# S4D convolution and gated linear unit on one core: which queues issue the output stores, and where the last Fourier stage stands

## The chip, the cores and the metric

The kernel runs on one core of a Trainium2 chip. The metric is device time in microseconds (us) of one execution, as a median over runs. Engines are called as in the profile: PE is TensorE's matmul, PEld its weight load, DVE is VectorE, ACT ScalarE, POOL GpSimd, SP SyncE. DMAs are issued by SP, ACT and POOL; a "q" behind an engine's name means its instruction queue (waits and DMA issues).

## The reference

The input has 2048 tokens of 448 channels. Both branches read the same layer-normalised input, and their outputs are added to the input:

```python
def _A_ref(u, log_A_real, A_imag, C_real, C_imag, log_dt, D_skip):
    ...
    P = jnp.exp((A * dt[:, None])[:, :, None] * pos[None, None, :])
    K = 2.0 * jnp.einsum("dn,dnl->dl", C, P).real
    Kf = jnp.fft.rfft(K, L2)
    Uf = jnp.fft.rfft(u_t, L2)
    y = jnp.fft.irfft(Uf * Kf[None, :, :], L2)[:, :, :L]
    return y + u * D_skip[None, None, :]

def _B_ref(x, w_gate, w_up, w_down):
    h = _sigmoid(einsum(x, w_gate)) * einsum(x, w_up)
    return einsum(h, w_down)

xn = _layernorm(x)
return x + _A_ref(xn, ...) + _B_ref(xn, ...)
```

A is a convolution over the whole sequence with a kernel K that is itself computed (448 channels, 256 states); B is a gated linear unit with 1792 inner features.

## The kernel before, in words

**Two streams, one order.** `conv()` does branch A and `glu()` branch B. Both are Python generators that write instructions and yield a cost; the loop at the end of the kernel always advances the stream that is behind by its share of the total, so their instructions are interleaved on every engine by those costs. `tc.issue_after` ties a group of matmuls behind the other stream's last one, which fixes the order on TensorE.

**Branch B (`glu`).** The 2048 tokens are 16 blocks of 128 (b 0 to 15), in two halves of eight. A half has two tiles of four blocks (t = 0, 1). For groups of two or three weight blocks f, `gate` (L710) multiplies tokens by the gate and up weights, ScalarE takes a tanh (`th`, L718), VectorE forms `hf` (L721), ScalarE rounds it to `hh` (L726), VectorE keeps the rest `hl`. Then come eight *down blocks*, one for each (t, b): nine matmuls for a group of three (`po`, L823) and one add into the accumulator on VectorE (`acc`, L828). In the second half GpSimd loads some of the weights and splits them in a high and a low part (`wh`, `wl` from `wraw`; `dh`, `dl` from `rdw`, L794 and L795). The accumulators of the first half go to DRAM and come back as `ac` (blocks 0 to 7); those of the second half are `accs[2]` (blocks 8 to 11) and `accs[3]` (12 to 15).

**Branch A (`spectra`).** The convolution is done by Fourier stages of 64 x 64, for the two halves of the channels apart (h = 0, 1: 224 columns each, H = 224). For each of 17 steps (h, k): `there` transforms kernel and input (`sp`, L904), ScalarE copies the kernel's part out of PSUM (`kc`, L912), VectorE multiplies (`yy`, `pd`, L915 to L918), `back` transforms back (`pv`, L931), ScalarE copies to `vt` (L937), which goes to DRAM (`v_d`) and returns in another layout (`vp`, L953). The loads of a step (`skl`, `sx`, `tb`) are issued by SP three steps ahead. `last(h, m)` is the last Fourier stage of a column half: 32 matmuls in the program (`pv`, L964; the two calls with m = 0, 2 or 4, 6 together are one row x64 in the trace) and adds into the accumulators (L972). m = 0, 2 finish `ac`, m = 4, 6 finish `accs[2]` and `accs[3]`. For h = 0 they are called in `spectra`, two in one step and two in the next. For h = 1 they are called in `glu`, between the last group's down blocks.

**Stores.** `out` (L234) writes four blocks and one column half by four DMAs of 32 partitions, 4 tokens and 224 columns (112 KB each). The issuing queue goes round: SP, ACT, POOL, by a counter (L238). The eight stores of `ac` for h = 0 are issued in the middle of the Fourier steps, all others at the end: h = 0 of `accs[2]` behind the down blocks of t = 0, then `ac` h = 1 behind `last(1, 0)` and `last(1, 2)`, `accs[3]` h = 0 behind the last down block, and at last `accs[2]` and `accs[3]` h = 1.

**Semaphores.** A DMA announces that it has landed on a semaphore. SP's and ACT's DMAs share eight of them (DMAHW0 to DMAHW7), POOL's have eight of their own (DMASW0 to 7). A DMA whose semaphore was used by an earlier one waits in its queue until that one has landed, and whatever is behind it in the queue waits too.

Of the kernel before, what the change touches and what calls it, by code (L numbers as in the profile page):

```python
# [20 lines left out]
D = 448  # L21
# [18 lines left out]
H = D // 2  # L40
# [90 lines left out]
def s4d_glu_kernel(ctx, tc, io):  # L131
    nc = tc.nc
# [4 lines left out]
    x_t, out_t = tok(io["A_u"][0]), tok(io["out"][0])  # L137
# [91 lines left out]
    accs = [acc_tile() for _ in range(2)]  # L229

    def blocks(t, g, b0, nb):
        return t[g, :, b0 // 8, b0 // 4 % 2, b0 % 4 : b0 % 4 + nb]

    def out(src, b0, h):  # L234

        ds = slice(H * h, H * h + H)
        for g in range(4):
            eng = (nc.sync, nc.scalar, nc.gpsimd)[outs[0] % 3]  # L238
            outs[0] += 1
            eng.dma_start(blocks(out_t, g, b0, 4)[:, :, ds], src[32 * g : 32 * g + 32, :, ds])  # L240

    def x_load(dst, b0, nb, engs):
        for g in range(4):
# [487 lines left out]
    def glu():  # L731
        for half in range(2):
# [4 lines left out]
            for fs_ in ORDER[half]:  # L737
# [3 lines left out]
                final = half == 1 and fs_ is ORDER[1][-1]  # L741
# [64 lines left out]
                for t in range(2):  # L806
                    acc = accs[2 * half + t]
                    for b in range(4):
                        if final and (t, b) == (0, 1):

                            yield None
                        if final and (t, b) == (1, 2):

                            sp_mm[:] = glu_mm
                            for m in (0, 2):
                                lasts[0](1, m)
                        po = psg.tile([128, D], F32, name="po", tag="gu", bufs=4)
                        bs = slice(128 * b, 128 * b + 128)
                        n = 0
# [13 lines left out]
                            step(*downs[t, b])  # L833
                    if cross:
                        nc.sync.dma_start(acc_d[:, 4 * t : 4 * t + 4], acc)
                    if final:
                        out(acc, 8 + 4 * t, 0)
                if final:
                    sp_mm[:] = glu_mm
                    for m in (4, 6):  # L840
                        lasts[0](1, m)
                    for t in range(2):
                        out(accs[2 + t], 8 + 4 * t, 1)

    def spectra(pf):

# [108 lines left out]
        def last(h, m):  # L955
# [13 lines left out]
            for b in range(2):  # L969
                q, o, ds = 2 * (m // 4) + b, m % 4, slice(H * h, H * h + H)  # L970
                acc = ac[:, 4 * q + o : 4 * q + o + 2, ds] if q < 2 else accs[q][:, o : o + 2, ds]
                v.tensor_tensor(acc, acc, pos[b], ALU.add)  # L972
# [135 lines left out]
            yield from spectra(pf)  # L1108

    turns = []  # L1110
    lasts, glu_mm, sp_mm, glu_on, outs, x1s, hfs, xls = [], [], [], [], [0], [0], [], []
# [45 lines left out]
```

## Time and profile before

| | |
|---|---|
| median of 3 runs | 721.07 us (721.0 to 723.01) |
| the profiled execution | 721.87 us, span 720.1 us |
| busy PE / PEld | 670.9 / 527.3 us (93% / 73% of the span) |
| busy DVE / ACT / POOL | 551.4 / 428.0 / 371.5 us (77% / 59% / 52%) |
| DMA | 117.23 MB, 163 GB/s over the span |

The span runs from the first to the last instruction; the execution's own time is 1.8 us longer. A row of the timeline has the start, the duration, engine, line, operation, output and inputs, the number of instructions merged in it, and in brackets the idle time ahead of it with what ended it. A row of the table of stretches has the stretch, its length, then busy time (and count) of PE, PEld, DVE, ACT and POOL, TensorE's granted clock, the busy share of the DMA engines and GB/s. A row of a line's instructions has durations as shortest/median/longest in ns, then the first and last start.

### The profile page before, as it was taken

The numbers are of one execution on the slowest core, as the hardware profiler recorded it, in microseconds if no ns is written. First come the engines' busy times: TensorE is split into PE (matmuls) and PEld (weight loads), VectorE is DVE, ScalarE is ACT, GpSimd is POOL, SyncE is SP. The second block draws the span as 40 slices with busy tenths as digits, with TensorE's granted clock in tenths as the row PEclk, the third lists the DMA queues.
The fourth block names the chain that finished last, engine by engine and source line by source line (L and its number), as shares of the span: only waits on it lengthen the run. The fifth ranks groups of instructions, "written<-read, shape, count | busy, mean of one in ns | idle before, by whom it ended". The sixth has DMA issues, their size and how long they took to land.

```text
span 720.1 us, 19127 instructions
## 1 busy us (share of the span) xinstructions
PE 670.9 (93%) x7752; PEld 527.3 (73%) x7752; DVE 551.4 (77%) x766; ACT 428.0 (59%) x678; POOL 371.5 (52%) x431
## 2 busy tenths in 40 slices
PE   3898999999997997989999999999999999998995
PEld 2676888877876875656888788877877777776783
DVE  5899988699899889985879889987946555546543
ACT  3655975677787789965686877777542322313320
POOL 2100147766987988885676687577833002251001
PEclk9999999999999999999999999999999999999998
DMA  9947374554254453647933344141359988899645
GB/s 208 238 118 215 97 214 154 166 159 153 64 168 140 135 135 107 178 136 203 257 112 95 95 132 128 46 140 43 86 162 319 216 235 231 253 290 228 172 131 152
DMA packets 94503, 117.23 MB, mean 163 GB/s; under 512 B 12752, under 2 KB 78288, under 8 KB 94416
## 3 DMA queue, kind: packets, MB, share of 16 engines
q1 hardware_dynamic: 65904, 91.87, 45.3%
q10 hardware_dynamic: 25936, 18.24, 9.5%
q0 software_dynamic: 2576, 5.90, 3.1%
q8 instruction: 61, 1.00, 0.6%
q14 instruction: 26, 0.21, 0.1%
HBM read 72.13 MB, written 43.84 MB: 161 GB/s over the span
## 4 chain that ended last, share of the span: by engine, by line
PE 42%; DVE 6%; ACT 4%; DMA 3%; issue 2%; SPq 1%; POOL 0%; POOLq 0%; DVEq 0%; ACTq 0%
PE gu L710 16%; PE po L823 9%; PE sp L904 6%; PE pv L931 4%; PE ko L616 4%; PE tr L542 2%; DVE Ft L604 1%; DMA sx<-x_d 1%; DVE Et L602 1%; DMA out_dram<-ac 1%; DVE Et L603 1%; PE kp L566 1%; ACT S L551 1%; ACT S L548 1%; SPq L492 1%
## 5 line engine op out<-in xcount | busy, mean ns | idle before, releaser
L520 POOL TENSOR_TENSOR me<-me,pm 128x32 f32<-128x32 f32 (+1 forms) x168 | 142.4, 848 | 73.4 <-DVE Et L603 62.1
L520 POOL TENSOR_TENSOR mf<-mf,pm 128x64 f32<-128x64 f32 (+1 forms) x112 | 119.7, 1069 | 5.9
L710 PE MATMUL gu<-xh,wh 128*128 128x512 f32 x336 | 100.0, 406 | 0.7 <-ACT xh L221 0.7
L710 PE MATMUL gu<-xh,wl 128*128 128x512 f32 x336 | 97.0, 395 | 0.0
L710 PE MATMUL gu<-xl,wh 128*128 128x512 f32 x336 | 95.8, 391 | 0.0
L602 DVE TENSOR_TENSOR Et<-me,S 128x1024 f32<-128x1024 f32 x56 | 81.8, 1461 | 17.2 <-ACT S L551 16.1
L603 DVE TENSOR_TENSOR Et<-me,S 128x1024 f32<-128x1024 f32 x56 | 78.0, 1394 | 12.6 <-ACT me L533 10.5
L823 PE MATMUL po<-dh,hh 128*128 128x448 f32 x224 | 84.2, 376 | 2.6 <-DVE hf L721 2.2
L823 PE MATMUL po<-dl,hh 128*128 128x448 f32 x224 | 82.3, 367 | 0.0
L604 DVE TENSOR_TENSOR Ft<-mf,S 128x1024 f32<-128x1024 f32 x56 | 78.1, 1394 | 5.4 <-ACT S L551 2.7
L548 ACT ACTIVATE S<-tr 128x1024 f32<-128x1024 f32 x56 | 57.6, 1028 | 40.8 <-PE tr L542 40.4
L823 PE MATMUL po<-dh,hl 128*128 128x448 f32 x224 | 81.2, 367 | 0.0
L616 PEld LDWEIGHTS ko<-Et,Ft 128*32 128x32 f32 x3584 | 55.2, 112 | 31.4 <-DVE Ft L604 13.3
L710 PEld LDWEIGHTS gu<-xh,wh 128*128 128x128 f32 x336 | 61.8, 191 | 20.1 <-issue 5.1
L616 PE MATMUL ko<-Et,Ft 128*32 128x64 f32 x3584 | 65.6, 224 | 10.8 <-DVE Ft L604 9.9
L710 PEld LDWEIGHTS gu<-xh,wl 128*128 128x128 f32 x336 | 63.8, 190 | 14.5 <-DVE hf L721 0.7
L710 PEld LDWEIGHTS gu<-xl,wh 128*128 128x128 f32 x336 | 63.4, 189 | 13.5
L726 ACT CAST hh<-hf 128x512 fp32r<-128x512 f32 x56 | 34.9, 623 | 61.8 <-DVE hf L721 57.7
L721 DVE SCALAR_TENSOR_TENSOR hf<-th,gu 128x512 f32<-128x512 f32 x56 | 38.1, 680 | 39.5 <-PE gu L710 27.1
L551 ACT ACTIVATE S<-S,hpi 128x1024 f32<-128x1024 f32 x56 | 65.5, 1170 | 0.0
L787 POOL TENSOR_TENSOR dl<-rd,dh 128x448 fp32r<-128x448 f32 x14 | 24.8, 1769 | 78.1 <-ACT dh L786 67.6
L828 DVE SCALAR_TENSOR_TENSOR acc<-po,acc 128x448 f32<-128x448 f32 x80 | 48.1, 615 | 20.7 <-PE po L823 20.4
(208 smaller groups left out, 1299.7 us busy)
## 6 DMA issues: line engine op xcount, KB each, us to landing
sk_d<-sk ACTq DMA_DIRECT2D x14, 512.0 KB
sx<-x_d SPq DMA_DIRECT2D x32, 224.0 KB
skl<-sk_d SPq DMA_DIRECT2D x16, 448.0 KB
vp<-v_d SPq DMA_DIRECT2D x16, 448.0 KB
v_d<-vt SPq DMA_DIRECT2D x14, 448.0 KB
ph<-ph_d SPq DMA_DIRECT2D x224, 24.0 KB
wt_d<-wh SPq DMA_DIRECT2D x9, 512.0 KB
wt_d<-wl SPq DMA_DIRECT2D x9, 512.0 KB
```

The costliest lines, as they stand in the source:

```text
L520: ins = nc.gpsimd.tensor_tensor(m[:, :, w + a : 2 * w : n], m[:, :, a:w:n], par(base + i).unsqueeze(2).to_broadcast([128, 4 * DC, w // n]) ...
L548: nc.scalar.activation(rows(cs), pv, AF.Abs)
L551: sins[:] = [nc.scalar.activation(cs, cs, AF.Sin, scale=-TWO_PI, bias=hpi)]
L602: v.tensor_tensor(Et[:, :, :, 32:64], two(me[:, :, 32:64]), S[:, 1::-1], ALU.mult)
L603: v.tensor_tensor(Et[:, :, :, 0:32], two(me[:, :, 0:32]), S[:, 1:3, :, ::-1], ALU.mult)
L604: fts[:] = [v.tensor_tensor(Ft, two(mf), S[:, 3:5], ALU.mult)]
L616: mm = nc.tensor.matmul(ko[32 * j : 32 * j + 32, sl], Ft[:, cc, DC * h + 4 * q + j], Et[:, cc, DC * h + 4 * q + j], start=(k == 0), stop=( ...
L710: glu_mm[:] = [nc.tensor.matmul(ps, a_, b_, start=(n == 0), stop=(n == len(mm) - 1))]
L721: marks[1] = v.scalar_tensor_tensor(hf, th, 1.0, pgu[1], ALU.add, ALU.mult)
L823: glu_mm[:] = [nc.tensor.matmul(po, a_[:, bs], w_, start=(n == 0), stop=(n == 3 * fc - 1))]
L828: v.scalar_tensor_tensor(acc[:, b], po, 0.5, acc[:, b], ALU.mult, ALU.add)
L904: mm = nc.tensor.matmul(to, tb[:kk, t, 64 * c : 64 * c + 64], rhs, start=True, stop=True, skip_group_check=True,)
```

## The change

`out` no longer goes round: it takes the range of blocks, the columns and the queues.

```diff
-    def out(src, b0, h):
-        ds = slice(H * h, H * h + H)
+    def out(src, b0, nb, ds, engs):
         for g in range(4):
-            eng = (nc.sync, nc.scalar, nc.gpsimd)[outs[0] % 3]
-            outs[0] += 1
-            eng.dma_start(blocks(out_t, g, b0, 4)[:, :, ds], src[32 * g : 32 * g + 32, :, ds])
+            eng = engs[g % len(engs)]
+            eng.dma_start(blocks(out_t, g, b0, nb)[:, :, ds], src[32 * g : 32 * g + 32, b0 % 4 : b0 % 4 + nb, ds])
...
-                        if final and (t, b) == (1, 2):
+                        if final and t == 1 and b >= 2:
                             sp_mm[:] = glu_mm
-                            for m in (0, 2):
+                            for m in (4 * b - 8, 4 * b - 6):
                                 lasts[0](1, m)
+                            if b == 3:
+                                out(accs[2], 8, 4, slice(H, D), (nc.sync, nc.scalar))
+                                out(accs[3], 12, 3, slice(0, D), (nc.sync, nc.scalar))
...
-                    if final:
-                        out(acc, 8 + 4 * t, 0)
-                if final:
-                    sp_mm[:] = glu_mm
-                    for m in (4, 6):
-                        lasts[0](1, m)
-                    for t in range(2):
-                        out(accs[2 + t], 8 + 4 * t, 1)
+                    if final and t == 0:
+                        out(acc, 8, 4, slice(0, H), (nc.gpsimd,))
+                    elif final:
+                        out(acc, 15, 1, slice(0, D), (nc.sync, nc.scalar))
...
                 for q in range(2):
-                    out(ac[:, 4 * q : 4 * q + 4], 4 * q, h)
+                    out(ac[:, 4 * q : 4 * q + 4], 4 * q, 4, ds, (nc.sync, nc.scalar) if h else (nc.gpsimd,))
```

The stores of column half 0 of `ac` and of `accs[2]` are issued by GpSimd alone, the others by SP and ACT in turn. `last(1, 4)` and `last(1, 6)` stand ahead of the last down block (t, b) = (1, 3); behind it only block 15 is left to store, with all its columns (four DMAs of 56 KB), and blocks 12 to 14 go out with all their columns as well (four of 168 KB). The lines below these places are two or three lower in the changed kernel (L240 is L238, L964 is L961).

On ScalarE (ACT), at the step in which `ac` is finished for h = 0, stood, with the semaphores that each instruction waits for:

```order
L912 COPY kc<-sp 128x448 [waits PE_49,Activation_49] x2
L240 DMA out_dram<-ac 32x4x224 [waits DMAHW4_49,DVE_49]
L240 DMA out_dram<-ac 32x4x224 [waits DMAHW7_49,DVE_49]
L240 DMA out_dram<-ac 32x4x224 [waits DMAHW1_49]
L718 ACTIVATE th<-gu 128x512 [waits PE_49]
L726 CAST hh<-hf 128x512 [waits DVE_49]
L937 COPY vt<-pv 128x2x224 [waits DMAHW2_49,PE_49]
```

and now stands:

```order
L909 COPY kc<-sp 128x448 [waits PE_49,Activation_49] x2
L716 ACTIVATE th<-gu 128x512 [waits PE_49]
L724 CAST hh<-hf 128x512 [waits DVE_49]
L934 COPY vt<-pv 128x2x224 [waits DMAHW2_49,DMAHW1_49,PE_49]
L934 COPY vt<-pv 128x2x224 [waits PE_49]
```

The three stores are gone, and `th`, `hh` and `vt` follow the copies `kc` directly. On GpSimd (POOL) at the same place and from there to the end, before:

```order
L648 DMA rdw<-in_B_w_down_dram 128x448 [waits Pool_49]
L240 DMA out_dram<-ac 32x4x224 [waits DMAHW4_49,DMAHW3_49,DVE_49]
L240 DMA out_dram<-ac 32x4x224 [waits DMAHW6_49,DMAHW5_49,DVE_49]
L794 CAST dh<-rdw 128x448 [waits DMASW2_49]
L795 TENSOR_TENSOR dl<-rdw,dh 128x448 [waits Pool_49]
L240 DMA out_dram<-acc 32x4x224 [waits DVE_49]
L240 DMA out_dram<-acc 32x4x224
L240 DMA out_dram<-ac 32x4x224 [waits DVE_49] x2
L240 DMA out_dram<-acc 32x4x224 [waits DVE_49]
L240 DMA out_dram<-acc 32x4x224
L240 DMA out_dram<-acc 32x4x224 [waits DMASW3_49,DVE_49]
L240 DMA out_dram<-acc 32x4x224 [waits DMASW4_49,DVE_49]
```

and now:

```order
L646 DMA rdw<-in_B_w_down_dram 128x448 [waits Pool_49]
L238 DMA out_dram<-ac 32x4x224 [waits DMAHW4_49,DMAHW3_49,DVE_49]
L238 DMA out_dram<-ac 32x4x224 x3
L238 DMA out_dram<-ac 32x4x224 [waits DMAHW6_49,DMAHW5_49,DVE_49]
L238 DMA out_dram<-ac 32x4x224 x2
L238 DMA out_dram<-ac 32x4x224 [waits DMASW2_49]
L792 CAST dh<-rdw 128x448
L793 TENSOR_TENSOR dl<-rdw,dh 128x448 [waits Pool_49]
L238 DMA out_dram<-acc 32x4x224 [waits DMASW3_49,DVE_49]
```

Eight stores instead of two stand ahead of the casts `dh` and `dl`, and the last of the eight takes over the wait for `rdw`. Behind `dl` GpSimd has four stores left (of `accs[2]`, h = 0) where it had eight, and none of them waits for the last Fourier stage. On ScalarE at the very end, where SP has the same rows, now stands:

```order
L238 DMA out_dram<-ac 32x4x224 [waits DMAHW7_49,DVE_49]
L238 DMA out_dram<-ac 32x4x224 [waits DMAHW1_49]
L238 DMA out_dram<-acc 32x4x224 [waits DMAHW2_49,DVE_49]
L238 DMA out_dram<-acc 32x4x224 [waits DMAHW5_49]
L238 DMA out_dram<-acc 32x1344 [waits DMAHW7_49,DVE_49]
L238 DMA out_dram<-acc 32x1344 [waits DMAHW1_49]
L238 DMA out_dram<-acc 32x448 [waits DMAHW3_49,DVE_49]
L238 DMA out_dram<-acc 32x448 [waits DMAHW5_49]
```

The two stores of block 15 (32x448) wait for the semaphores of stores of `accs[2]` that were issued eight DMAs earlier on the two queues. On TensorE the 32 rows of `last(1, 4)` and `last(1, 6)` stand nine matmuls further forward, between the last two down blocks.

More of the change, by code (lines that the diff above doesn't have):

```diff
@@ L1110, in s4d_glu_kernel @@
     turns = []
-    lasts, glu_mm, sp_mm, glu_on, outs, x1s, hfs, xls = [], [], [], [], [0], [0], [], []
+    lasts, glu_mm, sp_mm, glu_on, x1s, hfs, xls = [], [], [], [], [0], [], []
     xq, psc, raws, acl, marks, slots, pqs = list(x_first), [], [], [], [None, None], {}, []
```

## The prediction

> **What bounds the kernel now.** I read the page first, then TensorE's and ScalarE's timelines over the last 90 us, then the waits of the end. The page's head and its table of engines:
>
> ```profile
> span 720.1 us, 19127 instructions
> ...
> PE 670.9 (93%) x7752; PEld 527.3 (73%) x7752; DVE 551.4 (77%) x766; ACT 428.0 (59%) x678; POOL 371.5 (52%) x431
> ```
>
> TensorE is busy for 93% of the span, so a store matters only where it keeps TensorE waiting, or behind TensorE's last matmul. Both places exist. The first is the step in which the first Fourier half is finished. TensorE's timeline of an ordinary step with a `last` in it (from its `back`, line L931, at 631.55 to the next gate matmul, L710, at 639.09), then of the step after the stores:
>
> ```profile
> 631.55 1.78 PE L931 MATMUL pv<-yy,bk 64*128 64x224 f32 x16
> ...
> 639.09 0.97 PE L710 MATMUL gu<-xh,wh 128*128 128x512 f32 x3
> ...
> 644.31 1.78 PE L931 MATMUL pv<-yy,bk 64*128 64x224 f32 x16
> ...
> 650.36 0.98 PE L904 MATMUL sp<-skl,tb 128*64 128x224 f32 x8 [2.61 <-ACT vt L937]
> ...
> 654.38 0.96 PE L964 MATMUL pv<-vp,wf 64*32 64x224 f32 x16 [0.64 <-DVE pd L916]
> 655.27 0.96 PE L710 MATMUL gu<-xh,wh 128*128 128x512 f32 x3
> ```
>
> The brackets are idle time and what ended it: 2.61 us for ScalarE's copy `vt`, then 0.64 us for VectorE. Both steps run the same matmuls. The ordinary one takes 639.09 - 631.55 = 7.54 us, this one 655.27 - 644.31 = 10.96 us. ScalarE's timeline says why `vt` is late (its queue's DMA issues, taken from three narrow windows, then its instructions):
>
> ```profile
> 641.17 0.36 ACTq L240 DMA_DIRECT2D out_dram<-ac  x1
> ...
> 644.18 0.36 ACTq L240 DMA_DIRECT2D out_dram<-ac  x1
> ...
> 647.54 0.32 ACTq L240 DMA_DIRECT2D out_dram<-ac  x1
> 647.91 0.60 ACT L718 ACTIVATE th<-gu 128x512 f32<-128x512 f32 x1 [11.53 <-DMA out_dram<-ac]
> ...
> 649.79 0.96 ACT L937 COPY vt<-pv 128x448 f32<-128x448 f32 x2
> ```
>
> Three issues of about 0.35 us are spread from 641.17 to 647.86. Between them ScalarE's queue stands: the order shows a wait on a DMA semaphore (DMAHW7, DMAHW1) on the second and third store, that is, on the landing of an earlier transfer. `th`, `hh` and `vt` are queued behind. Was TensorE held by anything after that? One row of the table of stretches, 655.30 to 690.70:
>
> ```profile
> 655.30:690.70 35.40, 35.40 (x261) 26.64 (x258) 17.93 (x37) 11.69 (x22) 0.00 (x0) 1.00 0.77 179
> ```
>
> TensorE (second number) is busy for all 35.40 us at full clock (the 1.00), with the DMA engines 0.77 busy. So what is saved before 655 arrives in full at the down blocks.
>
> The second place is the end: TensorE's and VectorE's last instructions, the last issues of SP and ScalarE, then the rows of the kernel's closing line (L1153), where every engine waits for the others.
>
> ```profile
> 703.94 1.74 PE L964 MATMUL pv<-vp,wf 64*32 64x224 f32 x64
> 705.61 0.47 PE L823 MATMUL po<-dh,hh 128*128 128x448 f32 x1
> ...
> 707.33 0.37 PE L823 MATMUL po<-dh,hl 128*128 128x448 f32 x1
> ...
> 709.44 1.74 PE L964 MATMUL pv<-vp,wf 64*32 64x224 f32 x64
> ```
>
> ```profile
> 705.02 2.22 DVE L972 TENSOR_TENSOR ac<-ac,pv 128x448 f32<-128x448 f32 x4 [0.35 <-PE pv L964]
> 707.73 0.62 DVE L828 SCALAR_TENSOR_TENSOR acc<-po,acc 128x448 f32<-128x448 f32 x1 [0.50 <-PE po L823]
> 709.55 0.62 DVE L828 SCALAR_TENSOR_TENSOR acc<-po,acc 128x448 f32<-128x448 f32 x1 [1.20 <-PE po L823]
> 710.52 2.21 DVE L972 TENSOR_TENSOR acc<-acc,pv 128x448 f32<-128x448 f32 x4 [0.35 <-PE pv L964]
> ```
>
> ```profile
> 710.20 3.64 SPq L240 DMA_DIRECT2D out_dram<-acc  x4
> ```
>
> ```profile
> L1153 SPq EVENT_SEMAPHORE  x11: 17/28/3095, 713.9 to 720.0; - x11
> ...
> L1153 POOLq DRAIN  x3: 46/102/6277, 713.0 to 719.8; - x3
> L1153 SPq DRAIN  x3: 7/7/7, 717.8 to 719.6; - x3
> ...
> L1153 ACTq EVENT_SEMAPHORE  x2: 17/17/17, 719.5 to 720.0; - x2
> ```
>
> SP waits for the landings from 713.9 and has seen the last at 717.8, where its first DRAIN stands. GpSimd's first DRAIN begins at 713.0, right behind its last store, and the longest of the three lasts 6.28 us: to 719.3. The others are released at 719.5 and the span ends at 720.1. The end is thus set by GpSimd's own drain, 1.5 us behind the last landing, though no row of the chain of waits says so.
>
> **The change, part by part.**
>
> *The first half's stores leave SP and ScalarE.* ScalarE loses three issues with their waits, SP three. `th` can start when its matmuls end, `vt` when `pv` ends, as in the ordinary step, so the step should take 7.54 us: 10.96 - 7.54 = **3.4 us** saved on TensorE, the 2.61 us wait and what it drags behind it. Lower bound 2.6, the one wait that names ScalarE. More than 3.4 isn't there, since the rest of the step is matmuls that stay.
>
> SP's queue is relieved too: its next command, a `v_d` store, waits for `vt` anyway. The same 0.9 MB (8 x 112 KB) go through the same DMA engines, only later, so loads issued around 650 may land later; they fill buffers three steps ahead, and TensorE waited for none of them above. I take nothing for it.
>
> *GpSimd gets eight stores where it had two.* They stand behind the load of `rdw` and ahead of the casts `dh` and `dl`. GpSimd's timeline there, and the first matmul that uses the group's `dh` and `dl`:
>
> ```profile
> 647.33 1.16 POOL L240 DMA_DIRECT2D out_dram<-ac  x2
> 650.73 0.56 POOL L794 CAST dh<-rdw 128x448 fp32r<-128x448 f32 x1 [2.24 <-DMA rdw<-in_B_w_down_dram]
> 651.37 1.13 POOL L795 TENSOR_TENSOR dl<-rdw,dh 128x448 fp32r<-128x448 f32 x1
> ```
>
> ```profile
> 690.71 0.47 PE L823 MATMUL po<-dh,hh 128*128 128x448 f32 x1
> ```
>
> Two issues take 1.16 us, so eight take 4.6: 647.3 to 652.0. The adds they read were done before ScalarE's first store went out at 641.17, and `rdw`, for which the eighth waits, landed at 650.7. `dh` and `dl` end at about 653.7 instead of 652.5. They are needed at 690.7 - 3.4 = 687.3: cost nothing. The four stores of column half 0 of `accs[2]`, now all on GpSimd at 701.25 - 3.4, have nothing queued behind them but the drain.
>
> *The last Fourier stage moves ahead of the last down block.* No matmul is added. Worked in the old time, with 3.4 taken off at the end: the stage starts 0.30 after the last matmul of the block ahead of it begins (as before 709.44), so at 707.33 + 0.30 = 707.63. It takes 705.61 - 703.94 = 1.67, so the last block starts at 709.30. VectorE takes up a block's result 707.73 - 705.61 = 2.12 after its start: 711.42, done at 712.04. The old last result stands at 710.52 + 2.21 = 712.73. The four adds of the stage run from 707.63 + 1.08 = 708.71 to 710.92, ahead of that. So the last data is 0.7 earlier, and it is a quarter of the bytes of the old last batch: four stores of 56 KB, where eight of 112 KB were issued last.
>
> *GpSimd has no store at the end.* Its drain starts behind stores issued near 701 and, even at 6.28 us, ends long before SP's last wait. The end is then SP's last landing plus what followed the drain, 720.1 - 719.3 = 0.8. With unchanged landings that is 717.8 + 0.8 = 718.6, a gain of **1.5 us**.
>
> *The landings.* All 20 last stores now go through SP and ScalarE, whose DMAs share eight semaphores: the last four wait for the landing of the four stores of `accs[2]`. The trace has landing times for GpSimd's stores alone (of the rows on `out_dram`, the last 20 us):
>
> ```profile
> L240 POOL DMA_DIRECT2D out_dram<-acc x6: 551/551/551, 701.2 to 713.0; - x6
> ...
> DMA to landing us min/median/max: 2.7/3.2/4.1
> ```
>
> The third add of the stage ends 0.5 before the fourth, so `accs[2]` is issued from 710.4 and, at two issues a queue, until 711.0. Two landings follow one another from there: 711.0 + 2 x 2.7 = 716.4 at the shortest, 711.0 + 2 x 4.1 = 719.2 at the longest, 717.4 with the median. Since the last stores move half of what those rows moved I take 717.1, that is **0.7 us** earlier than 717.8 (bounds 1.4 either way). The old end agrees in size: SP's last issue ends at 710.20 + 3.64 = 713.84, and 717.8 is 4.0 behind it.
>
> Sum: 3.4 + 1.5 + 0.7 = **5.6 us**, between 2.6 + 1.5 - 1.4 = 2.7 and 3.4 + 1.5 + 1.4 = 6.3. The profiled execution took 721.87 (span 720.1 and 1.8 around it) and would take 716.3. The median of the runs is 721.07, 0.8 below it, and would be **715.5**.
>
> **A rule against it.** ScalarE's three issues together are 1.04 us; the other 5.65 us of its 6.69 are waits. The Trainium skill, "DMA: Bandwidth & Descriptors", section "Issuing engines are not separate DMA queues", says that spreading DMAs over issuing engines saves only the sequencer's initiation time, usually small beside the DMA. By that rule ScalarE gets 1.04 us back, off TensorE's path, and the first term is nothing. The trace disagrees, as its 11.53 us row shows, if what holds ScalarE goes with the stores.
>
> **The rivals.**
>
> *The wait moves (6 in 100).* If ScalarE was late because the DMA engines were full, the full engines remain: `vt` also waits for an earlier `v_d` store to land, and could take the wait over. Then only the end pays: 1.5 + 0.7 = 2.2, time 718.9. For it: full queues held the stores. Against: `vt` reuses one of two buffers, stored a whole step before, and TensorE's 35.40 busy microseconds show no such wait. The quoted rule gives this time too.
>
> *The semaphores of the end bite (17 in 100).* With landings at the slow bound, 719.2, the end is 720.0 in old time: 1.5 - 1.4 = 0.1 gained there, 3.5 in all, time 717.6. For it: twelve stores queue within 4 us and the last four wait for earlier ones. Against: the last are half as large.
>
> *GpSimd becomes late (4 in 100), the slower case.* If its stores are issued slowly, `dl` of the last weight block holds the down blocks. GpSimd has 687.3 - 647.3 = 40 us for eight issues and 1.7 us of casts: from 4.8 us an issue TensorE waits. At 6 us an issue it is 48 + 1.7 - 40 = 9.7 late, less the 5.6: 4.1 slower, 725.2. Against: two issues took 1.09 us while VectorE added (its four adds end at 707.24):
>
> ```profile
> 706.99 1.09 POOL L240 DMA_DIRECT2D out_dram<-ac  x2 [4.65 <-DVE ac L972]
> ```
>
> For such a slowing speaks the Trainium skill, "SBUF — State Buffer", section "A bandwidth-pool intuition that's wrong (but worth ruling out)": a DMA issued from GpSimd can stand until VectorE gives up the port they share, since GpSimd can't write descriptors meanwhile, and one that takes some 0.62 us alone took 3.1. The row above doesn't show that; an estimate by the page's 3.1 us gives 24.8 us for eight, still inside the 40.
>
> **How the numbers follow.** The forecast has 73 in 100, at 715.5. A measurement of this kernel tells 0.3%, 2.2 us, from no change. Forecast and semaphore rival are faster by more: 0.90. The moved wait, 718.9, is counted as the same: 0.06. GpSimd late: 0.04. The range runs from the sum's far bound, 721.07 - 6.3 = 714.8, less 0.6 because a store of 56 KB may land sooner than any in those rows, to its near bound, 721.07 - 2.7 = 718.4: 714.2 to 718.4, which holds the first two cases.
>
> **What would show it.** Right: no idle of TensorE for `vt` near 647 and `th` of ScalarE right after its matmuls; the step 7.5 us long; GpSimd's drain over by 710 and SP last at the end; the last stores issued behind a semaphore wait. Wrong: a wait of TensorE over 1 us between 641 and 690, `dl` later than 687, or a last landing later than 3.4 us ahead of 717.8. The forecast falls if the span is over 717.5.

## The result and the profile after

| | before | changed |
|---|---|---|
| median of 20 runs each, same chip | 723.12 us (718.24 to 728.2) | 719.19 us (715.83 to 723.97) |
| ratio, 95% interval | | 0.9941 [0.9923, 0.9959] |
| the profiled execution | 721.87 us, span 720.1 | 716.67 us, span 714.9 |

The change is faster by 3.9 us between the medians, 4.3 us by the ratio (3.0 to 5.6). Forecast were 5.6 us and 715.5 us. The kernel before, run 20 times, lies 2.05 us above the median of three from which the forecast was taken.

Both profiled executions reach the step of the first half's stores at the same time (`pv` at 644.31 and 644.16), so their traces can be laid side by side there. TensorE in the changed kernel, the ordinary step and the one of the stores (L928 is the old L931, L961 the old L964, L708 the old L710):

```profile
631.41 1.78 PE L928 MATMUL pv<-yy,bk 64*128 64x224 f32 x16
...
638.95 0.96 PE L708 MATMUL gu<-xh,wh 128*128 128x512 f32 x3
...
644.16 1.78 PE L928 MATMUL pv<-yy,bk 64*128 64x224 f32 x16
...
651.21 0.96 PE L961 MATMUL pv<-vp,wf 64*32 64x224 f32 x16 [0.44 <-DVE pd L913]
652.10 0.96 PE L708 MATMUL gu<-xh,wh 128*128 128x512 f32 x3
...
654.82 1.78 PE L928 MATMUL pv<-yy,bk 64*128 64x224 f32 x16
```

The step from `pv` to the gate takes 652.10 - 644.16 = 7.94 us instead of 10.96. The 2.61 us for `vt` are gone, 0.44 us for VectorE's `pd` is left. ScalarE has `th` and `vt` as early as the prediction says, and GpSimd issues its eight stores at 0.55 us each ahead of the casts:

```profile
641.78 0.60 ACT L716 ACTIVATE th<-gu 128x512 f32<-128x512 f32 x1 [5.53 <-PE gu L708]
...
645.98 0.97 ACT L934 COPY vt<-pv 128x448 f32<-128x448 f32 x2 [0.30 <-PE pv L928]
```

```profile
645.26 4.38 POOL L238 DMA_DIRECT2D out_dram<-ac  x8
649.63 0.78 POOL L792 CAST dh<-rdw 128x448 fp32r<-128x448 f32 x1
650.50 1.13 POOL L793 TENSOR_TENSOR dl<-rdw,dh 128x448 fp32r<-128x448 f32 x1
```

`th` no longer waits 11.53 us for a store, and `dl` is over at 651.63, far ahead of 687. The end: VectorE's last results, the issues of SP, and the closing line.

```profile
705.53 2.21 DVE L969 TENSOR_TENSOR acc<-acc,pv 128x448 f32<-128x448 f32 x4 [0.35 <-PE pv L961]
708.25 0.62 DVE L829 SCALAR_TENSOR_TENSOR acc<-po,acc 128x448 f32<-128x448 f32 x1 [0.51 <-PE po L824]
```

```profile
707.24 4.44 SPq L238 DMA_DIRECT2D out_dram<-acc  x6
```

```profile
L1150 SPq EVENT_SEMAPHORE  x11: 17/28/28, 711.7 to 714.8; - x11
...
L1150 POOLq DRAIN  x3: 46/93/5360, 699.5 to 714.6; - x3
L1150 SPq DRAIN  x3: 7/7/7, 714.1 to 714.4; - x3
```

The order of the last two rows of VectorE is turned round, its last result stands at 708.87. GpSimd's drain runs from 699.5 for 5.36 us, to 704.8, and SP's first DRAIN at 714.1 is now what the other engines wait for; the span ends 0.8 later. Before, the same chain was 717.8 for SP, 719.3 for GpSimd's drain, 720.1 for the end.

Between these two executions that is 3.0 us in the step, 0.7 in VectorE's last result and 1.5 in the drain, 5.2 in all, close to the 5.6 forecast. Yet the medians differ by 3.9. What one execution shows isn't what the kernel does as a rule, and the experiments had to find where.

### The profile page after: what moved, and what is told of

It is laid out like the page before. It is cut to its first block, busy times and chain, and to the rows that moved or that the text cites. A ratio compares the mean times of both kernels' runs of the same rounds, so it can differ in the third digit from the quotient of the medians.

```text
span 714.9 us, 19123 instructions
## 1 busy us (share of the span) xinstructions
PE 668.8 (94%) x7752; PEld 525.4 (73%) x7752; DVE 556.9 (78%) x766; ACT 428.2 (60%) x678; POOL 377.6 (53%) x433
## 4 chain that ended last, share of the span: by engine, by line
PE 65%; DVE 16%; ACT 6%; issue 4%; POOL 4%; SPq 2%; DMA 2%; ACTq 0%; DVEq 0%; POOLq 0%
PE gu L708 28%; PE po L824 15%; PE sp L901 7%; PE ko L614 5%; PE pv L928 4%; PE tr L540 3%; DVE Ft L602 3%; DVE Et L601 2%; DVE Et L600 2%; POOL me L518 2%; ACT S L549 1%; POOL mf L518 1%; ACT S L547 1%; DVE hl L726 1%; PE kp L564 1%
## 5 line engine op out<-in xcount | busy, mean ns | idle before, releaser
L518 POOL TENSOR_TENSOR me<-me,pm 128x32 f32<-128x32 f32 (+1 forms) x168 | 146.2, 870 | 70.9 <-DVE Et L601 59.5
L708 PE MATMUL gu<-xh,wh 128*128 128x512 f32 x336 | 98.6, 401 | 1.6 <-ACT xh L221 1.0
L708 PE MATMUL gu<-xh,wl 128*128 128x512 f32 x336 | 96.6, 393 | 0.0
L708 PE MATMUL gu<-xl,wh 128*128 128x512 f32 x336 | 96.0, 392 | 0.0
L600 DVE TENSOR_TENSOR Et<-me,S 128x1024 f32<-128x1024 f32 x56 | 82.8, 1479 | 15.5 <-ACT S L549 14.8
L601 DVE TENSOR_TENSOR Et<-me,S 128x1024 f32<-128x1024 f32 x56 | 79.3, 1415 | 11.1 <-ACT me L531 11.1
L708 PEld LDWEIGHTS gu<-xh,wh 128*128 128x128 f32 x336 | 60.6, 188 | 20.8 <-issue 5.1
L708 PEld LDWEIGHTS gu<-xh,wl 128*128 128x128 f32 x336 | 63.4, 189 | 14.3 <-DVE hf L719 0.7
L708 PEld LDWEIGHTS gu<-xl,wh 128*128 128x128 f32 x336 | 63.4, 189 | 13.5
L785 POOL TENSOR_TENSOR dl<-rd,dh 128x448 fp32r<-128x448 f32 x14 | 26.3, 1877 | 79.3 <-ACT dh L784 68.8
```

The lines of the kernel that those rows point to most:

```text
L518: ins = nc.gpsimd.tensor_tensor(m[:, :, w + a : 2 * w : n], m[:, :, a:w:n], par(base + i).unsqueeze(2).to_broadcast([128, 4 * DC, w // n]) ...
L600: v.tensor_tensor(Et[:, :, :, 32:64], two(me[:, :, 32:64]), S[:, 1::-1], ALU.mult)
L601: v.tensor_tensor(Et[:, :, :, 0:32], two(me[:, :, 0:32]), S[:, 1:3, :, ::-1], ALU.mult)
L708: glu_mm[:] = [nc.tensor.matmul(ps, a_, b_, start=(n == 0), stop=(n == len(mm) - 1))]
```

## The experiments

Theory A is the prediction's sum: ScalarE's stores hold `th` and `vt`, GpSimd's drain sets the end, the rest is small. Theory B: TensorE is granted less of its clock in the changed kernel, and that takes part of the gain back. Beside the ratio to the kernel before, the table has the mean span at one clock. In the runs of one kernel the span rises by 4.8 us for each 0.01 of mean granted clock that an execution lacks (one slope fitted within all kernels); with it each run's span was brought to a clock of 0.98 and the mean taken. This halves the scatter, from 2.3 to 1.1 us; what stands behind ± is the standard error of the mean; it also removes what a kernel gains by keeping TensorE's clock up.

The column has a fault when kernels with different ends are compared. The mean clock is taken over the whole span, and behind TensorE's last matmul the clock stands at 0.50 with nothing for TensorE to do: for the last 6.0 us of the profile before, and for the last 3.1 us of the changed one. A stretch of each:

```profile
715.00:717.00 2.00, 0.00 (x0) 0.00 (x0) 0.00 (x0) 0.00 (x0) 0.00 (x0) 0.50 0.77 248
```

```profile
712.00:714.00 2.00, 0.00 (x0) 0.00 (x0) 0.00 (x0) 0.00 (x0) 0.00 (x0) 0.50 0.37 113
```

In the profiles this stretch lasts 5.0 us on the mean in the six executions with the old end (before, c0_before, d1_before, d2_before, a_first, one_store) and 3.0 us in seven with the new one (changed, after_again, t_tail, t_one, s_sponly, l_late, w_quiet). 2.0 us at half clock are 0.0014 of the mean clock, 0.7 us by the slope. So the column shows a kernel with the new end some 0.7 us too slow against the kernel before; this is an estimate. Kernels with the same end can be compared as they stand.

| kernel | median us | ratio to before [95%] | span at clock 0.98 |
|---|---|---|---|
| before (128 runs on four chips) | 721.71 to 723.74 | | 721.2, 721.2, 721.2, 721.6 (each ±0.2 to 0.3) |
| changed | 719.19 | 0.9941 [0.9923, 0.9959] | 718.65 ±0.15 |
| after_again | 719.76 | 0.9968 [0.994, 0.9995] | 719.06 ±0.29 |
| c0_before | 723.74 | 1.0014 [0.9989, 1.0038] | 721.19 ±0.41 |
| a_first | 722.25 | 1.0006 [0.9975, 1.0036] | 720.70 ±0.34 |
| b_nopool_end | 720.80 | 0.9983 [0.9955, 1.0012] | 719.75 ±0.35 |
| t_tail | 721.98 | 0.9983 [0.9957, 1.0009] | 721.02 ±0.33 |
| one_store | 722.40 | 0.9989 [0.9969, 1.001] | 720.13 ±0.29 |
| t_one | 720.64 | 0.9975 [0.9951, 0.9999] | 719.24 ±0.29 |
| s_sponly | 719.44 | 0.9968 [0.9945, 0.9991] | 719.04 ±0.25 |
| n_drain | 721.24 | 0.9965 [0.9939, 0.999] | 719.95 ±0.17 |
| p_sem | 721.98 | 1.0 [0.9972, 1.0028] | 720.72 ±0.17 |
| w_quiet | 719.21 | 0.9961 [0.993, 0.9993] | 719.04 ±0.23 |
| wp | 723.13 | 1.0009 [0.9978, 1.0041] | 721.21 ±0.22 |
| l_late | 719.70 | 0.9946 [0.9919, 0.9973] | 718.69 ±0.22 |
| v_early | 719.92 | 0.9957 [0.9938, 0.9976] | 718.11 ±0.31 |

The mean granted clock of the runs is 0.979 to 0.982 for the kernel before, and 0.9825 (changed) and 0.9821 (after_again) for the changed one, so theory B has nothing for it. Theory A doesn't get its number either: it expected a line about 5 us below that of the kernel before, and at one clock the changed kernel lies 2.5 to 2.6 us below the kernel before, 3.2 to 3.3 with the 0.7.

### How large is the stall of the step?

The kernel before, unchanged, profiled three more times; c0_before was also run twelve times.

> The kernel before, unchanged, as one of the kernels compared, for its scatter and its granted clocks. Theory A (the change takes out 5.2 us as the two traces have it, and the level of the runs, which moves by several us with the stretches at half clock, is what the prediction missed): ratio 1.000, times between 718 and 728, and its spans rise as the granted clock falls, along a line that lies about 5 us above that of the changed kernel at the same number of half-clock stretches. Theory B (with fewer pauses TensorE is granted less clock, so part of the gain is given back in most runs): the same times, but granted clocks that are higher on the whole than those of the changed kernel, and a line less than 5 us above it.

> The kernel before, unchanged, one execution. If the landing of the fifth load ahead of ScalarE's third store sets the loss, the third store is issued 0.02 us after an sx load has landed, and the step (pv to the next pv, 10.28 us without a stall) is longer than 10.28 by the time from the start of pv to that issue plus 0.2 to 0.4 us: 1 to 3.4 us. If the loss had another cause, the two would not go together.

> The same once more. With the four executions so far (1.0, 1.5, about 3, 3.4 us) the mean loss should lie near 2.2 us; if both new ones lose over 3 us, the 3.4 us of the prediction was the rule, and the missing time is somewhere else.

TensorE's waits in its list for 641 to 712 us, of the first and then of the second of them:

```profile
PE sp L904 <- ACT vt L937: 0.7, 1, 0.7
PE pv L964 <- DVE pd L916: 0.7, 1, 0.7
```

```profile
PE sp L904 <- ACT vt L937: 3.3, 1, 3.3
```

The same code waits 0.7 us for `vt` in one execution and 3.3 us in another. What sets the size is one load. ScalarE's third store waits for the semaphore of an `sx` load, and in every execution it goes out 0.02 us after that load has landed by the trace: 647.52 and 647.54 in the profile before, then 648.47 and 648.49, 649.30 and 649.32, 647.97 and 647.99 in the three new ones. That load is issued 7.7 to 7.8 us ahead of `pv` each time and takes 8.4 to 11.7 us; the busy share of the DMA engines is 1.03 to 1.06 from 636 to 648 us of the profile before. For all six executions with the old placement of these stores (b_nopool_end and t_tail, below, have it too), with the loss as the time from `pv` to VectorE's last result over that of an undisturbed execution (64.3 us in the new order of the end: after_again and s_sponly have no wait there and take 64.31 and 64.32; 65.0 in the old order, an estimate, one_store's 65.84 less its one wait of 0.87):

| execution | `pv` starts | third store issued | later than `pv` by | loss, us |
|---|---|---|---|---|
| b_nopool_end | 646.37 | 647.03 | 0.66 | 1.0 |
| c0_before | 647.20 | 648.49 | 1.29 | 1.5 |
| d2_before | 645.73 | 647.99 | 2.26 | 2.6 |
| before, as predicted from | 644.31 | 647.54 | 3.23 | 3.4 |
| t_tail | 650.58 | 654.12 | 3.54 | 4.1 |
| d1_before | 645.39 | 649.32 | 3.93 | 4.7 |

The loss goes with the landing. Up to 0.8 us of it is TensorE's other wait in the step, for VectorE's `pd`: in b_nopool_end, where the third store is early, that wait of 0.77 us is the only one in the step. Why the same load takes 8.4 us in one execution and 11.7 in another wasn't tried and stays open. The mean loss is 2.9 us, where d2_before's expectation had 2.2, and it is 0.3 us (0 to 0.9) over nine executions in which ScalarE issues none of these stores: the changed kernel, after_again, s_sponly, n_drain, l_late, v_early, w_quiet, p_sem and wp. In d1_before and t_tail the wait has an extra price, seen in TensorE's timeline of d1_before and in its table of stretches (the third number from the end is the clock):

```profile
647.10 0.98 PE L904 MATMUL sp<-skl,tb 128*64 128x224 f32 x8
647.91 0.93 PE L904 MATMUL sp<-sx,tb 128*64 128x224 f32 x8
652.14 1.74 PE L904 MATMUL sp<-skl,tb 128*64 128x224 f32 x8 [3.31 <-ACT vt L937]
653.67 1.71 PE L904 MATMUL sp<-sx,tb 128*64 128x224 f32 x8
```

```profile
652.00:654.00 2.00, 1.85 (x10) 1.24 (x12) 1.39 (x3) 0.98 (x4) 1.60 (x2) 0.55 0.38 144
654.00:656.00 2.00, 2.00 (x32) 1.14 (x36) 1.35 (x4) 0.51 (x1) 0.09 (x1) 0.59 0.79 195
```

Behind the wait TensorE has a clock of 0.55 and 0.59 over 4 us, and the same eight matmuls take 1.74 us instead of 0.98. So a wait of 3.3 us cost 4.7, more than d1_before's expectation allowed. Behind the 2.61 us of the profile before the clock stayed at 1.00.

### Which store does it?

One store of the 32 is moved: the third of ScalarE's, in the old kernel (one_store) and in the changed kernel with the old rotation (t_one).

```diff
 # one_store, from the kernel before
             eng = (nc.sync, nc.scalar, nc.gpsimd)[outs[0] % 3]
+            eng = nc.gpsimd if outs[0] == 7 else eng
 # t_tail, from the changed kernel: the queues in spectra's two calls (q) of out
-(nc.sync, nc.scalar) if h else (nc.gpsimd,)
+(nc.sync, nc.scalar) if h else ((nc.sync, nc.scalar, nc.gpsimd), (nc.scalar, nc.gpsimd, nc.sync))[q]
 # t_one: as t_tail, but for the eighth store
+(nc.sync, nc.scalar) if h else ((nc.sync, nc.scalar, nc.gpsimd), (nc.scalar, nc.gpsimd, nc.sync, nc.gpsimd))[q]
```

> The changed kernel with the first half's stores going round SP, ScalarE and GpSimd again. Theory A: the step after the stores takes 11 us again, the end stays as in the changed kernel, so 1.5 + 0.7 = 2.2 us faster than before, span about 717.9 in a run with the same half-clock stretches, ratio 0.997. Theory B: a median nearer to before, ratio 0.998 to 0.999.

> The kernel before, with one edit: the third of ScalarE's stores of the first half is issued by GpSimd; the other nineteen places stay. If that one wait is the loss, th runs right after its matmuls or after the second store, the step is 10.3 to 10.8 us, and the time falls by up to 2.2 us, less what the last vp load then costs (2.0 us in the kernel with all eight on GpSimd): ratio 0.997 to 1.0. If the bytes or SP's waits are the loss, the step is still over 11 us.

> The changed kernel with the first half's stores in the old rotation, but for that same third store, which GpSimd issues. If it is the whole loss, this equals the changed kernel (ratio 0.993 to 0.997, step under 10.9 us). If SP's stores or the full engines matter as much, it equals the kernel with the whole rotation (ratio 0.998).

ScalarE in t_one, where two stores are left:

```profile
648.89 2.51 ACTq L238 DMA_DIRECT2D out_dram<-ac  x2
651.44 0.60 ACT L716 ACTIVATE th<-gu 128x512 f32<-128x512 f32 x1 [8.76 <-DMA v_d<-vt]
```

`th` still waits behind the second store, for a `v_d` store to land, but that is over in time: TensorE's only wait in the step is 0.55 us for `pd`, and 0.87 us in one_store. At one clock t_one is 1.8 us under t_tail and within 0.2 to 0.6 us of the changed kernel. That is the third store's wait: SP's three stores and the bytes are the same in both. The ratios alone don't show it (0.9975 and 0.9983, intervals overlapping). In the old kernel the same move brings less, 1.1 us at one clock (±0.4), and one_store's step takes 11.10 us from `pv` to `pv`, not the 10.3 to 10.8 expected; by its expectation's own sign that spoke for the bytes or SP's waits, but what is over an undisturbed step's 10.28 is the one wait for `pd`, and TensorE has none for `vt`.

### Can the time saved in the step be lost again?

All eight stores on GpSimd, the rest as before; on SP alone in the changed kernel; and in the changed kernel behind `dl` or held back to 682 us by a copy on GpSimd.

```diff
 # a_first, from the kernel before
+            eng = nc.gpsimd if outs[0] < 8 else eng
 # s_sponly, from the changed kernel
-(nc.sync, nc.scalar) if h else (nc.gpsimd,)
+(nc.sync, nc.scalar) if h else (nc.sync,)
 # w_quiet, from the changed kernel, in the last group at (t, b) == (0, 0), cut; the call in
# spectra is left out for h == 0. l_late does the same behind dl instead of the copy
+jk_ = nc.gpsimd.tensor_copy(jk, hs[0][-1][1][:, 0:1])
+with tc.issue_after(jk_.ins):
+    for q in range(2):
+        out(acl[0][:, 4 * q : 4 * q + 4], 4 * q, 4, slice(0, H), (nc.gpsimd,))
```

> The kernel before with the first half's eight stores on GpSimd alone and nothing else changed. Theory A: the step after the stores takes 7.9 us instead of 10.96, the end stays as it was (GpSimd's drain sets it), 3.0 us faster, ratio 0.996. Theory B: the same profile, but a median only 1 to 2 us lower, ratio 0.998. Rival (the wait moves to a transfer): TensorE idles for vt or a load in the steps up to 690 and the profile is under 1 us shorter.

> The changed kernel with the first half's eight stores on SP alone: neither ScalarE nor GpSimd issues them. Theory A (ScalarE's standing queue is the cost): TensorE's wait for vt stays away, and the 0.4 us wait for VectorE too, since GpSimd issues nothing there: the step takes 7.5 to 7.6 us, span 714.5. SP's queue stands instead, its vt store goes out up to 3 us later, and the loads behind it have over 10 us to spare. Rival (full DMA engines, whichever queue): a wait of over 2 us for vt or a load in this step or the next two, 2 to 4 us slower than the changed kernel.

> The changed kernel with GpSimd's eight stores behind its casts dh and dl instead of ahead of them. If the 0.4 us that is left of TensorE's wait comes from GpSimd's work beside VectorE's multiplications in the same step, the stores now run 650 to 654.5 and the casts ahead of them, and the wait changes by up to 0.4 us either way; the total stays within 1 us of the changed kernel by every theory.

> The changed kernel with GpSimd's eight stores of the first half held back to about 687 us, when the DMA engines are least busy (a copy of one column on GpSimd stands ahead of them). Theory 'bytes': the 0.9 MB that the stores put into a stretch with full DMA engines delay the chain of v_d stores and vp loads and hold VectorE back; then the 0.4 us wait goes, the last vp load lands 2 us or more ahead of the last Fourier stage instead of 1.3, and the time is 0.4 us or more below the changed kernel's. Theory 'queues': only where the stores stand in a queue matters; then the time is within 0.4 us of the changed kernel's, ratio to the kernel before 0.992 to 0.996.

a_first has the step without a wait (10.28 us from `pv` to `pv`) and a gain of only 0.5 us at one clock (±0.4), none by the ratio: in its profile TensorE waits later, as the rival in its expectation had it. Its timeline at the last Fourier stage of h = 1 (its first half), and SP's last loads:

```profile
706.22 1.75 PE L965 MATMUL pv<-vp,wf 64*32 64x224 f32 x64 [2.01 <-issue]
```

```profile
695.37 0.54 SPq L954 DMA_DIRECT2D vp<-v_d  x1
696.00 0.57 SPq L948 DMA_DIRECT2D v_d<-vt  x1
701.21 0.54 SPq L954 DMA_DIRECT2D vp<-v_d  x1
701.85 0.59 SPq L241 DMA_DIRECT2D out_dram<-acc  x1
```

The last `vp` load waits for its `v_d` store, which lands at 701.20, goes out at 701.21 and lands at 706.13 by the trace; TensorE was ready 2.0 us earlier. The bracket doesn't name the load; that it is what TensorE waits for is read from the 0.09 us between its landing and the row. SP issues each `vp` load when its `v_d` store has landed. The last of these stores took 5.2 us in a_first and 2.5 us in the profile before. The slack of that load ahead of the last Fourier stage is 1.5 us in before and c0_before, 1.3 in the changed kernel and in v_early, 1.0 in l_late, 0.5 in n_drain, 0.4 in s_sponly, 0.1 in p_sem. A gain of 2 to 3 us in the step is thus not far from the point where this chain takes it back, and in a_first it passed it.

SP alone does as well as GpSimd (0.4 us apart at one clock, errors 0.25 and 0.15): it isn't GpSimd that matters but that ScalarE is rid of the waits. l_late and w_quiet equal the changed kernel: when the 0.9 MB go out changes nothing that can be measured (each of these means is good to 0.2 or 0.3 us), and the theory of the bytes falls. In w_quiet TensorE even waits 0.95 us for `pd`, and its last `vp` load lands 1.1 us ahead, not 2.

### The end

GpSimd out of the last twenty stores of the old kernel (b_nopool_end; its expectation says sixteen, but the edit takes all from the thirteenth on, of which GpSimd had six); one of the last four given to it in the changed kernel (n_drain); column half 1 of `accs[2]` given to it (p_sem; wp is p_sem and w_quiet together); column half 0 of blocks 12 to 14 stored ahead of the last stage (v_early).

```diff
 # b_nopool_end, from the kernel before
+            eng = (nc.sync, nc.scalar)[outs[0] % 2] if outs[0] >= 12 else eng
 # n_drain
-out(acc, 15, 1, slice(0, D), (nc.sync, nc.scalar))
+out(acc, 15, 1, slice(0, D), (nc.sync, nc.scalar, nc.gpsimd))
 # p_sem
-out(accs[2], 8, 4, slice(H, D), (nc.sync, nc.scalar))
+out(accs[2], 8, 4, slice(H, D), (nc.gpsimd,))
 # v_early
-out(accs[3], 12, 3, slice(0, D), (nc.sync, nc.scalar))
+out(accs[3], 12, 3, slice(H, D), (nc.sync, nc.scalar))
+if final and (t, b) == (1, 2):                                # behind the add
+    out(acc, 12, 3, slice(0, H), (nc.gpsimd,))
```

> The kernel before with the last sixteen stores on SP and ScalarE in turn, none of them on GpSimd behind the last results; the order of the stages stays. Theory A: GpSimd's drain is over early and SP's last wait sets the end, 1.5 us faster in the profile, ratio 0.998; against it the four stores that GpSimd no longer issues lengthen the two queues, by at most 1 us. If the drain is no cost of its own: no change.

> The changed kernel with one of the last four stores (56 KB of block 15) issued by GpSimd. Theory A: the end is set by GpSimd's drain again, about 2.3 us behind the landing of its store instead of 0.1 us behind SP's last wait, so 1 to 2 us longer than the changed kernel. If the drain is not what held the end: within 0.5 us of it.

> The changed kernel with column half 0 of blocks 12 to 14 stored by GpSimd right behind down block (1, 2), so that the four late stores of these blocks carry half of their columns. Theory A, with the end bound by the bytes that are still to move behind the last adds: 344 KB of 1.38 MB leave the tail, about 1 us earlier, if GpSimd's drain (2.3 us behind its last landing, near 708) is over before SP's last wait, near 713. If the tail is bound by semaphores and latency: no change.

> The changed kernel with the four stores of column half 1 of accs[2] issued by GpSimd, so that the last four stores no longer wait for semaphores of that batch. Theory 'semaphores': the last four are issued 0.8 us earlier (at 708.9 for 709.7 in that kernel's time) and SP sees the last landing 0.8 us earlier after VectorE's last add, 4.4 us for 5.2. Theory 'landing': the landing comes about 5 us behind VectorE's last add whatever the issue waits for. In both GpSimd's drain begins late again: its last landing near 712 and 2.4 us more, about 0.3 us behind SP's, so the time is 0 to 1 us above the changed kernel's.

> Both edits together, the stores at 687 us and column half 1 of accs[2] on GpSimd. By the theories 'queues' and 'landing' this is 0 to 1 us above the changed kernel; by 'bytes' and 'semaphores' it is 0.4 to 1 us below it.

> The changed kernel once more, unchanged, as the mark for the three kernels beside it. If the first half's stores cost TensorE an amount that differs between executions of the old code (1.0 to 3.4 us in four executions) and nearly nothing in the new, the step again has no wait over 0.5 us (pv to the next pv under 10.8 us), the last vp load again lands about 1 us ahead of the last Fourier stage, and the ratio is 0.994 as before (0.992 to 0.996). If the new code has the stall too, only more rarely, the step is 11 us or longer here.

The closing line of n_drain, then of p_sem:

```profile
L1150 POOLq DRAIN  x3: 46/93/6562, 713.4 to 720.5; - x3
L1150 SPq DRAIN  x3: 7/7/7, 718.5 to 720.2; - x3
```

```profile
L1150 POOLq DRAIN  x3: 46/93/8061, 711.7 to 720.3; - x3
L1150 SPq DRAIN  x3: 7/7/7, 718.4 to 720.0; - x3
```

In n_drain GpSimd's drain ends at 713.4 + 6.56 = 720.0, 1.5 us behind SP's 718.5, where the span of the kernel before had 719.3 against 717.8. One 56 KB store is enough; at one clock it costs 1.3 us, and by the profile, from VectorE's last result to the end, 7.6 us instead of 6.1. b_nopool_end shows the other side: its span ends 5.7 us behind VectorE's last result, where the kernel before has 7.2 on the mean, and it is 1.4 to 1.5 us lower than before at one clock (±0.4, and 0.7 more if the estimate above holds for it); its ratio, 0.9983, doesn't tell it from no change. p_sem has the same 1.4 us and a second loss: VectorE's last result is at 711.67 and SP's last landing 6.7 us behind it, where it is 5.2 in the changed kernel. The last issues of SP in p_sem:

```profile
710.57 3.20 SPq L238 DMA_DIRECT2D out_dram<-acc  x4
```

They end at 713.77, 2.1 us behind VectorE's last result; in the changed kernel it was 707.24 + 4.44 = 711.68, 2.8 behind. So the last four stores do go out earlier, by about the time expected, and yet the last landing comes later. The theory of the semaphores has the landing wrong; but GpSimd's four stores of `accs[2]` also go out later than SP's and ScalarE's did, so what the semaphore waits alone cost is not shown. p_sem and wp give back 1.7 and 2.2 us against after_again and w_quiet, more than the 0 to 1 us expected. v_early is level with the changed kernel (ratio 0.9957 and 0.9941, intervals overlapping; half a microsecond lower at one clock, within two errors): the landing comes 5.1 us behind VectorE's last result whether blocks 12 to 14 go out with 168 or 84 KB a store.

The time from VectorE's last result to the end of the span, over the executions: 7.37, 7.57, 6.96 and 6.83 us in the kernel before, 6.03 and 6.09 in the changed one. So the end as a rule gives 1.1 us there and 0.7 for the earlier result, 1.8 where 2.2 were forecast: SP's last landing stands 4.6 to 5.3 us behind VectorE's last result before (mean 4.9) and 5.2 after.

after_again is the changed kernel once more, and it shows why single spans mislead: its `pv` row of the step is

```profile
650.20 1.78 PE L928 MATMUL pv<-yy,bk 64*128 64x224 f32 x16
```

6.0 us later than in the other execution of the same code, with no wait in the step and 64.31 us from there to VectorE's last result. Its span is 720.6 us against 714.9. The difference lies in stretches of half clock before 350 us, 27.3 us of them against 13.7, ahead of everything that the change touches. Its step and its slack of 1.0 us are as expected, its ratio is not: 0.9968, a gain of 2.3 us (0.4 to 4.3), where 0.992 to 0.996 was expected.

t_tail has the whole new end (its span ends 6.1 us behind VectorE's last result) and the old stores of the first half. 1.8 us were due, and a ratio of 0.997 was expected; at one clock it is 0.2 us below the kernel before, 0.9 with the 0.7, each ±0.4, and its ratio doesn't tell it from no change.

## Why the prediction was wrong, point by point

*Stores leave SP and ScalarE, 3.4 us.* The mechanism was right: `th` and `vt` follow their matmuls, and t_one against t_tail shows that the wait of the third store is what held them long enough to matter. The size was the step that failed: "so the step should take 7.54 us: 10.96 - 7.54 = 3.4 us saved" took one execution's wait for the kernel's. Six executions lose 1.0 to 4.7 us, on the mean 2.9 ±0.6, and 0.3 is left: 2.6 us. The lower bound of 2.6 was no bound, since it came from the same row, and "More than 3.4 isn't there" was none either: in d1_before the matmuls behind the wait ran at half clock. A wait that ends with the landing of a load has the spread of that landing, here over 3 us of latency.

*Loads that land later, nothing.* Right for the changed kernel, by 1.3 us of slack that was not looked up; a_first, the same stores with the old end, lost 2.0 us there.

*GpSimd's eight stores, nothing.* Right: 0.55 us each, `dl` over 35 us early. The row that the prediction gave against the slower case shows little, since its two issues from 706.99 stand beside VectorE's adds only until 707.24; after_again, where all eight do, shows it.

*The drain, 1.5 us.* Right, by n_drain and b_nopool_end, and by the four profiles of the kernel before, where GpSimd's drain ends 1.4 to 1.5 us behind SP's first.

*The landings, 0.7 us.* VectorE's last result is 0.7 us earlier as worked out, but the last landing follows it by 5.2 us and not by the 4.9 that the old end has on the mean. 0.4 us is left.

Sum: 2.6 + 1.5 + 0.4 = 4.5 us where 5.6 were forecast; the ratio has 4.3 (3.0 to 5.6). That the two agree so well is in part luck: after_again has 2.3 (0.4 to 4.3), and at one clock the gain is 2.5 to 2.6, or 3.2 to 3.3 with the estimate of 0.7. The parts alone come to less as well, 1.1 for one_store and 0.2 (0.9 with the 0.7) for t_tail. So the terms as the traces have them may be 1 us more than the runs give; where that us goes isn't shown.

Taking the 4.5 us, of the 3.7 us between 715.5 and 719.19, 1.1 are these two terms and 2.05 the step "The median of the runs is 721.07, 0.8 below it, and would be 715.5": three runs of a kernel whose runs scatter from 718 to 728. The remaining 0.5 is within the interval of the ratio. The larger part of the miss is thus the starting point, and the step that failed in the sum is the size of its first term. The range held neither scatter: it was made of the bounds of the sum alone, and the error of its starting point, over 1 us for three such runs, was left out; "over 1 us" is an estimate from their spread.

*The rule against it*, by which the first term would be nothing, is not borne out here: s_sponly and the changed kernel gain over t_tail by 2.0 to 2.4 us at one clock though ScalarE's issues are 1.04 us together, and t_one gets most of that from one issue of 0.32 us.

*The rivals.* The moved wait did not come for `vt` in the changed kernel, but in a_first it came for `vp`, at another load and 50 us later. That full DMA engines did it, as the prediction has it, isn't shown: their busy share there is 0.57 to 0.64 from 690 to 705 us. GpSimd was not late. The semaphores of the end: the last landing is 5.2 us behind VectorE's last result in the new end and 4.9 in the old; how much of the 0.3 is semaphore waits, p_sem doesn't tell.

## What to carry to other kernels

A DMA issue that waits on a semaphore of an earlier, unrelated load holds everything behind it on that engine for as long as that load takes to land: look for the wait, not for the length of the issue, and move the one issue that has it. A wait of that kind must be sized from several executions, since its end is a landing in a crowd of transfers; and the time from which a forecast starts must come from more than three runs where runs scatter by 10 us. A clock averaged over the whole span counts the end too, where TensorE has nothing to do, so it misleads when a change moves the end. And an engine that issues DMAs near the end pays with its drain at the end of the kernel, so the last stores belong on queues whose drain is short.

## What the runs showed of the hardware

TensorE's clock falls to half for 3.4 us, or two or three times that, behind some waits and not behind others: behind 3.31 and 2.92 us in d1_before and t_tail, not behind 2.61 us in the profile before, but behind 1.59 us in that same execution, at 494 us:

```profile
494.08 1.10 PE L616 MATMUL ko<-Et,Ft 128*32 128x64 f32 x64 [1.59 <-DVE Ft L604]
```

```profile
494.00:496.00 2.00, 1.82 (x81) 1.62 (x82) 1.06 (x2) 1.31 (x2) 0.00 (x0) 0.92 0.15 37
496.00:498.00 2.00, 2.00 (x6) 1.52 (x6) 2.00 (x3) 1.90 (x4) 0.59 (x1) 0.50 0.08 23
```

In the changed kernel's profile a wait of 1.72 us at the same place left the clock at 1.00. The Trainium skill, "TensorE: Matmul & The Clock Gate", section "What's actually happening", has the gate judge TensorE by a window of some 3.4 us that runs freely. By this the same gap can fall within one window or across two, which would make it a matter of chance. The traces agree with the chance and with the length (stretches of 3.41, 6.83 and 10.24 us); the idle window of 3.4 us that the Trainium skill asks for there before the clock falls is not what the 1.59 us show. An execution meets three to six such stretches while TensorE works, and the number and length of them make most of the 8 to 10 us between runs of one kernel.

GpSimd's drain at the end lasts until 2.0 to 2.5 us behind the landing of its last store (landed 702.44, drained 704.84 in the changed kernel), and is from 4.7 to 8.1 us long in all.

VectorE's short operations on SBUF can take longer beside GpSimd's making of `dl`, and with them comes the 0.3 to 0.9 us for `pd` that is left in some executions. VectorE and GpSimd in w_quiet:

```profile
655.28 0.47 DVE L920 TENSOR_TENSOR yy<-yy 128x224 f32<-128x224 f32 x1
655.78 1.22 DVE L921 TENSOR_TENSOR yy<-pd 128x224 f32<-128x224 f32 x1
```

```profile
655.59 1.16 POOL L793 TENSOR_TENSOR dl<-rdw,dh 128x448 fp32r<-128x448 f32 x1
```

L921 takes 1.22 us beside `dl`, 0.39 without it. In after_again, where GpSimd issues its eight stores during the same operations (652.37 to 656.74), they take 0.38 us. The split isn't clean: in the changed kernel's profile L914 takes 0.78 us beside the last of the eight stores (at 648.80) and 0.89 us beside `dl` (at 650.98), and in after_again L915 takes 0.38 us beside `dl` (at 657.46), which itself takes 1.35 us instead of 1.13.
